# Retention values and the next unit's scores in one run of 64-row matmuls, with the values' results in the banks of the first products

## The chip, the cores and the metric

The kernel runs on one core of one Trainium2 chip. The metric is the device time of one execution in microseconds. A core has TensorE (PE in the rows, its weight loads PEld), VectorE (DVE), ScalarE (ACT), GpSimd (POOL) and SyncE (SP), which issues most DMAs here. Each engine works through its own queue in program order. TensorE writes only to PSUM, which has eight banks of 2 KB for each of its 128 partitions.

## The reference, cut to what matters

```python
scores = scale * np.matmul(q, k.transpose(0, 1, 3, 2))      # 4 x 8 heads, 576 tokens, dim 64
ret = scores * Dmat                                         # decay gamma**(i - j), causal
attn_out = np.matmul(ret, v)
x = attn_out.transpose(0, 2, 1, 3).reshape(2304, 512)
h = x @ w_in;  x = (h * sigmoid(h)) @ w_out                 # first layer, 512 -> 2048 -> 512
h = x @ w_in2; out = np.maximum(h, 0) ** 2 @ w_out2         # second layer
```

All of it is float32.

## The kernel before, in words

The 2,304 tokens are 18 units of 128. The retention of a unit is computed in chunks of 64 tokens: scores inside a chunk, a running state from chunk to chunk, and the values from both. Units 0 to 3 come first, by themselves. The other fourteen (4 to 17) are computed beside the first layer's ordinary products, which run in three blocks of 512, 384 and 384 tokens (j = 0, 1, 2). The remaining tokens and the second layer follow later with other products.

The first layer of one block is a loop over sixteen slices f of the hidden dimension. For each f, `gemm1` issues twelve 128x128 matmuls into one bank `ph`, ScalarE takes the Silu of it (line 743) and rounds it (745), VectorE forms the rest (746), and two slices later `gemm2` adds twelve matmuls into the four banks `acc`. So TensorE's order is gemm1(f), gemm2(f-2), gemm1(f+1), gemm2(f-1), and so on. A product keeps float32 precision by three matmuls for each pair: high by high, high by low, low by high.

The loop's body is cut into half steps n = 2f and n = 2f+1. At an even n the queue of TensorE stands between gemm1(f) and gemm2(f-2); at an odd n it stands between gemm2(f-2) and gemm1(f+1). In each half step the weights' conversion comes first (`conv_step` in block 0, `pre_step` in block 1: ScalarE's lines 126, 127 and 194, VectorE's 179, 182, 130 and 199), then `flush()`, which issues what the lists `later` and `behind` hold (the Silu at an even n, line 746 at an odd one), then gemm2 at an odd n, then `run_att`. ScalarE's order in an even half step of block 0 is therefore: the rounding of a converted weight (194), which waits for VectorE's line 130, and then the Silu.

`run_att` spreads two kinds of steps over the half steps by a proportion. `scores_step(u)` issues 64 matmuls on 64x64 tiles into the tile `P` (lines 442 and 446), then the state's additions (475, 477), the scaling of the queries (458) and the mask (450). `values_step(u)` issues 48 or 64 such matmuls into `Q` (496, 498, 504), copies one part of the result (506), and leaves the additions (527, 529 or 518, 520), the rounding (530) and the low part (534) for the next flushes. It then scales the keys of the next unit (`prep_k`: POOL's line 428 for the first half of the heads, four ScalarE instructions of line 431 for the second) and loads unit u+2 (line 406, from SP's queue).

In PSUM, `ps_a` has one tile of two banks, which `P` and `Q` take in turn; `ps_g` has two tiles of one bank, which the successive `ph` take in turn; `ps_o` has the four of `acc`.

```python
        at = behind if u < u_end[2] else later
        at.append(lambda: (whole(), at.append(low)))
...
                run_att(a0 + (a1 - a0) * (2 * f + odd + 1) // (27, 29, 22)[j])
```

With these numbers the steps of block 0 stand at n = 4 (scores of 4), 8 (values of 4), 13 (scores of 5), 17 (values of 5), 22 (scores of 6) and 26 (values of 6); those of block 1 at 4, 9, 14, 19, 24 and 28; those of block 2 at 1, 2, 4, 5, 6, 8, 9, 10, 12, 13, 15, 16, 17, 19, 20 and 21.

Of the kernel before, what the change touches and what calls it, by code (L numbers as in the profile page):

```python
# [7 lines left out]
F32 = mybir.dt.float32  # L8
# [15 lines left out]
NU = NCH  # L24
# [5 lines left out]
LAG = 2  # L30
W1_FIRST, SINGLES = 4, 6
HALVED = (7, 9)
AHEAD = 256
HALF = (slice(0, 64), slice(64, 128))
WARM = 5
# [8 lines left out]
def kernel(  # L44
# [147 lines left out]
    def pair_c(n, parts=slice(0, 2)):  # L192
        cols = slice(512 * parts.start, 512 * parts.stop)
        nc.scalar.copy(flat(tiles_of(*pairs[n - SINGLES])[0])[:, cols], conv[n][0].bitcast(F32)[:, cols])
# [8 lines left out]
    later = []  # L203
    behind = []
# [23 lines left out]
    def conv_step(n):  # L228
# [14 lines left out]
        if odd:  # L243
            if first < q <= end:
                parts = slice(1, 2) if q - 1 in HALVED else slice(0, 2)
                pair_c(q - 1, parts)
# [8 lines left out]
        if first < q <= end:  # L255
            if q - 1 in HALVED:
                for e in range(2):
# [87 lines left out]
    u_end = [sum(BLOCKS[: j + 1]) // C for j in range(len(BLOCKS))] + [NU]  # L345
# [3 lines left out]
    n_start = BLOCKS[0] // C  # L349
# [43 lines left out]
    def att_psum(name, pool=ps_a, tag="a"):  # L393
        return pool.tile([128, 2, 512], F32, tag=tag, name=name)

    def new_raw(u):
        if u < n_start:
            raw[u] = [wp.tile([128, 1024], F32, tag="w", name="raw") for _ in range(NG)]
        else:
            raw[u] = [ap.tile([128, 1024], F32, tag="raw", name="raw") for _ in range(NG)]  # L400

    def load(u, queue=nc.sync):
        if u < NU:
            new_raw(u)
            for g in range(NG):
                queue.dma_start(out=raw[u][g], in_=att[NG * u + g])
# [6 lines left out]
    def toks(u, a, e, b, first):  # L413

        c0 = first + (2 * a + e) % 4 * D
        return raw[u][a // 2][HALF[b], c0 : c0 + D]

    def place(u, b):

        return (2 * u + b) % PER  # L420

    def prep_k(u):

        for g in range(NG):
            kn = raw[u][g][:, 256:512].rearrange("p (h d) -> p h d", h=4)
            w = (Tkn_u if u < n_start else Tkn)[:, 4 * g : 4 * g + 4]
            if u == n_start or g == 0:
                nc.gpsimd.tensor_mul(kn, kn, w.unsqueeze(2).to_broadcast([128, 4, D]))
            else:
                for h in range(4):  # L430
                    nc.scalar.activation(kn[:, h], kn[:, h], ACTF.Copy, scale=w[:, h : h + 1])
# [3 lines left out]
    def scores(u):  # L435

        P_of[u] = P = att_psum("P")
        for a in range(4):
            for e, b in FOUR:
                if place(u, b) < PER - 1:  # L440
                    o = P[HALF[e], b, 256 + a * D : 256 + a * D + D]
                    mm(o, toks(u, a, e, b, 256), toks(u, a, e, b, 512), start=True, stop=True)  # L442
        for a in range(4):
            for e, b in FOUR:
                o = P[HALF[b], e, a * L : a * L + L]
                mm(o, dims(u, a, e, b, 768), dims(u, a, e, b, 0), start=True, stop=True)  # L446
# [10 lines left out]
            w = Tq[:, 2 * g : 2 * g + 2].unsqueeze(2).to_broadcast([128, 2, 2 - b0, L])  # L457
            nc.gpsimd.tensor_mul(q, q, w)

    def scores_step(u):  # L460
        scores(u)
        new_state(u, 0)
        scale_q(u)
        mask(u)
        new_state(u, 1)
# [17 lines left out]
    def values(u):  # L483


        Q = att_psum("Q")
        o = Q[:, 0].rearrange("p (a t) -> p a t", a=4)
        x1 = Q[:, 1, 0:256].rearrange("p (a t) -> p a t", a=4)
        rf = rf_t.pop(u)
        states = [b for b in range(2) if place(u, b)]  # L490
        for a in range(4):
            for e, b in FOUR:
                v = toks(u, a, e, b, 512)
                if e == b:
                    w = o[HALF[e], a, b * L : b * L + L]
                    mm(w, v, rf[HALF[b], e, a], start=a == 0, stop=a == 3 and not states)  # L496
                else:
                    mm(x1[HALF[e], a], v, rf[HALF[b], e, a], start=True, stop=True)
        for b in states:
            for a in range(4):  # L500
                for e in range(2):
                    sg = S_at[2 * u + b][HALF[e], a]
                    w = o[HALF[e], a, b * L : b * L + L]
                    mm(w, sg, dims(u, a, e, b, 0), start=False, stop=a == 3 and b == states[-1])  # L504
        xs = ap.tile([128, 4, L], F32, tag="xs", name="xs", bufs=1)
        nc.scalar.copy(xs, x1)
        xh, xl = x_part(u)
        raw.pop(u)
        if xl is None:
            for e, p in enumerate(HALF):  # L510
                nc.scalar.copy(xh[p, :, e * L : e * L + L], o[p, :, e * L : e * L + L])

        def into_x():
            for e, p in enumerate(HALF):
                b = 1 - e
                t = slice(b * L, b * L + L)
                if place(u, b):
                    nc.vector.tensor_add(xh[p, :, t], o[p, :, t], xs[p])
                else:
                    nc.vector.tensor_copy(xh[p, :, t], xs[p])  # L520

        def whole():
            for e, p in enumerate(HALF):
                b = 1 - e
                oc = o[p, :, b * L : b * L + L]
                if place(u, b):
                    nc.vector.tensor_add(oc, oc, xs[p])
                else:
                    nc.vector.tensor_copy(oc, xs[p])
            nc.scalar.copy(xh, o)  # L530

        if xl is None:
            return into_x, lambda: None
        return whole, lambda: nc.vector.tensor_sub(xl, o, xh)

    def values_step(u):
        whole, low = values(u)
        at = behind if u < u_end[2] else later
        at.append(lambda: (whole(), at.append(low)))
        if u + 1 < NU:  # L540
            prep_k(u + 1)
        load(u + 2)

# [230 lines left out]
    low = behind  # L776
# [422 lines left out]
    load_w(SINGLES)  # L1199

    first_units()
    att_steps = [(u, step) for u in range(n_start, NU) for step in (scores_step, values_step)]
    pos = [0]

    def run_att(upto):
        while pos[0] < min(upto, len(att_steps)):
            u, step = att_steps[pos[0]]
            step(u)
            pos[0] += 1

    def att_end(j):
        return 2 * (u_end[j] - n_start)

    su_ctx.close()
    ps_g, ps_o = (
        ps_ctx.enter_context(
            tc.tile_pool(name=nm, bufs=n, space=bass.MemoryType.PSUM, reuse_waits="tile")
        )
        for nm, n in (("ps_g", 2), ("ps_o", 4))
    )  # L1220
# [51 lines left out]
    for i in range(len(seq) + LAG):  # L1272
        if i < len(seq):
            layer, j, f = seq[i]
            if i == 0:
                for c in ((0, AHEAD), (AHEAD, BLOCKS[0])):
                    for ff in range(2):
                        gemm1(layer, j, ff, *c)
            elif i > 1:
                gemm1(layer, j, f)  # L1280
            if i == 0:
                for n in range(W1_FIRST):
                    keep_w(n)
            if i == 1:
                load(n_start + 1)
        for odd in range(2):
            if i == 0 and not odd:
                cut_consts(2)
            step = 2 * (i - (nb - 1) * KF) + odd
            if step >= 0:  # L1290
                flush()
            if i < len(seq):
                if j == 0:
                    conv_step(2 * f + odd)
                if j == 1 or step == 0:
                    pre_step()
                if j == 1 and odd == 0:
                    nc.sync.dma_start(out=woD[f // 2, f % 2], in_=w_pair[1, f // 2][f % 2].bitcast(F32))
            if step < 0:
                flush()  # L1300
            if odd and i >= LAG:
                gemm2(*seq[i - LAG])
            if i < len(seq):
                a0, a1 = att_end(j), att_end(j + 1)
                run_att(a0 + (a1 - a0) * (2 * f + odd + 1) // (27, 29, 22)[j])
                if j == nb - 1:
                    for p in range(5):
                        ts_step(p, step - 4 * p - 3)
            if step >= 0:
                strassen_x(step)  # L1310
    flush()
    flush()
    low = later
# [34 lines left out]
    for n in range(2 * KF):  # L1348
        h, f = divmod(n, KF)
# [11 lines left out]
        low = behind  # L1361
        last_block(n)
        low = later
# [55 lines left out]
    for n, (P, i) in enumerate(order2):  # L1419
# [8 lines left out]
        else:  # L1428
            at = 3 if P == 1 else 0
# [11 lines left out]
    low = []  # L1441
# [93 lines left out]
```

## Time and profile before

| | |
|---|---|
| median of three runs | 816.18 us (815.82 to 816.43) |
| the profiled execution's own time | 816.38 us |
| its span, first to last instruction | 814.6 us |
| outside the span | 1.8 us |
| TensorE busy | 805.3 us, 99% of the span |
| VectorE, ScalarE, POOL busy | 67%, 53%, 25% |
| granted TensorE clock, mean | 1.000 |

The blocks with the fourteen units lie between about 26 us and 290 us of the span; block 0 ends at about 120 us and block 1 at about 198 us. TensorE's busy time counts matmuls that overlap in its pipeline, so the order and the starts of its instructions tell more than that share.

### The profile page before, as it was taken

How to read it: one execution, taken by the hardware profiler on the slowest of the kernel's cores; microseconds unless marked ns; L12 is line 12 of the kernel's file. 1: busy time of each engine (PE TensorE's matmuls, PEld its weight loads, DVE VectorE, ACT ScalarE, POOL GpSimd, SP SyncE). 2: the span in 40 equal slices, each digit the busy share in tenths (PEclk: the TensorE clock that was granted, in tenths of full speed). 3: DMA queues.
4: the chain of work that ended last, by engine and by line, in shares of the span. 5: the costliest groups of instructions: out<-in, count | busy, mean ns of one | idle time of the engine just before them, and what ended most of it. 6: DMA issues, size and time to landing. Idle time of an engine off the chain costs nothing.

```text
span 814.6 us, 16076 instructions
## 1 busy us (share of the span) xinstructions
PE 805.3 (99%) x6426; PEld 747.6 (92%) x6426; DVE 545.6 (67%) x783; ACT 434.3 (53%) x797; POOL 202.6 (25%) x224
## 2 busy tenths in 40 slices
PE   7999999999999999999999999999999999999998
PEld 6887889999999988888888999999999999999998
DVE  5999975454455566575787676536566988777772
ACT  5787755444454445454455575645568644333330
POOL 3402202424566122223431222402355000000000
PEclk9999999999999999999999999999999999999999
DMA  9976555896552032788794565353488744433300
GB/s 352 393 283 231 211 199 197 313 325 240 196 193 95 2 117 93 257 312 286 228 358 159 172 216 162 129 169 105 149 306 280 283 166 153 138 133 133 107 27 27
DMA packets 73307, 160.69 MB, mean 197 GB/s; under 512 B 6032, under 2 KB 37520, under 8 KB 73232
## 3 DMA queue, kind: packets, MB, share of 16 engines
q1 hardware_dynamic: 68480, 151.28, 53.3%
q10 hardware_dynamic: 4752, 8.39, 2.8%
q8 instruction: 50, 0.82, 0.4%
q14 instruction: 25, 0.20, 0.1%
HBM read 104.07 MB, written 55.57 MB: 196 GB/s over the span
## 4 chain that ended last, share of the span: by engine, by line
PE 91%; issue 3%; DVE 2%; ACT 1%; POOL 0%; DVEq 0%; POOLq 0%; ACTq 0%
PE acc L83 23%; PE pa L1092 13%; PE pa L1001 12%; PE ph L83 11%; PE pb L1092 10%; PE pb L1001 9%; PE pa L860 5%; PE pb L860 4%; PE Q L504 1%; PE P L442 1%; PE Q L496 1%; PE P L446 1%; DVE t L130 0%; ACT t L126 0%; DVE t L143 0%
## 5 line engine op out<-in xcount | busy, mean ns | idle before, releaser
L1092 PE MATMUL pa<-w2s,gl 128*128 128x256 f32 x864 | 108.1, 283 | 0.0
L1001 PE MATMUL pa<-xa,w1s 128*128 128x384 f32 x576 | 106.0, 336 | 0.0
L1092 PEld LDWEIGHTS pa<-w2s,gl 128*128 128x128 f32 x864 | 105.7, 192 | 0.0
L1001 PEld LDWEIGHTS pa<-xa,w1s 128*128 128x128 f32 x576 | 100.5, 188 | 0.1
L83 PE MATMUL acc<-gsl,wo 128*128 128x512 f32 x384 | 87.4, 390 | 0.0
L83 PEld LDWEIGHTS acc<-gsl,wo 128*128 128x128 f32 x384 | 72.1, 188 | 15.2
L790 ACT CAST gl<-gr 128x1024 fp32r<-128x1024 f32 (+1 forms) x57 | 55.7, 1002 | 52.1 <-DVE gr L1066 25.3
L1092 PE MATMUL pb<-w2s,gl 128*128 128x256 f32 x648 | 82.0, 283 | 0.0
L1001 PE MATMUL pb<-xa,w1s 128*128 128x384 f32 x432 | 81.1, 336 | 0.0
L1092 PEld LDWEIGHTS pb<-w2s,gl 128*128 128x128 f32 x648 | 79.6, 192 | 0.0
L1001 PEld LDWEIGHTS pb<-xa,w1s 128*128 128x128 f32 x432 | 75.5, 188 | 0.4 <-DVE u L1013 0.4
L83 PE MATMUL ph<-xh,wih 128*128 128x384 f32 (+2 forms) x200 | 70.8, 354 | 0.7 <-ACT sg L743 0.7
L791 DVE TENSOR_TENSOR gl<-gr,gl 128x1024 fp32r<-128x1024 f32 (+1 forms) x55 | 64.4, 1179 | 8.0 <-ACT gl L790 8.0
L83 PE MATMUL acc<-gh,woh 128*128 128x384 f32 (+1 forms) x192 | 69.3, 361 | 0.0
L83 PE MATMUL ph<-xl,wih 128*128 128x384 f32 (+2 forms) x200 | 69.2, 346 | 0.0
L83 PE MATMUL ph<-xh,wil 128*128 128x384 f32 (+2 forms) x200 | 69.2, 346 | 0.0
L83 PE MATMUL acc<-gh,wol 128*128 128x384 f32 (+1 forms) x192 | 67.9, 354 | 0.7 <-DVE wol L199 0.7
L83 PE MATMUL acc<-gl,woh 128*128 128x384 f32 (+1 forms) x192 | 67.8, 353 | 0.0
L746 DVE TENSOR_TENSOR gl<-sg,gh 128x384 fp32r<-128x384 f32 (+1 forms) x48 | 31.5, 658 | 45.9 <-ACT gh L745 45.9
L743 ACT ACTIVATE sg<-ph 128x384 f32<-128x384 f32 (+1 forms) x48 | 25.2, 524 | 62.9 <-PE ph L83 62.0
L126 ACT ACTIVATE t<-wr 128x512 f32<-128x512 f32 x64 | 42.7, 667 | 22.4 <-DMA wr<-w 18.2
L1013 DVE TENSOR_TENSOR u<-pb,s 128x384 f32<-128x384 f32 x48 | 26.0, 553 | 31.9 <-PE pb L1001 31.6
(156 smaller groups left out, 1514.2 us busy)
## 6 DMA issues: line engine op xcount, KB each, us to landing
wr<-w SPq DMA_DIRECT2D x64, 512.0 KB, 5.9
gD<-g SPq DMA_DIRECT2D x48, 384.0 KB, 2.7
gr<-gD SPq DMA_DIRECT2D x36, 512.0 KB, 4.4
raw<-att SPq DMA_DIRECT2D x34, 512.0 KB, 4.9
wo<-woD SPq DMA_DIRECT2D x16, 512.0 KB, 6.4
w2r<-w2c SPq DMA_DIRECT2D x14, 512.0 KB, 6.0
xq<-x SPq DMA_DIRECT2D x12, 384.0 KB, 5.2
out<-y ACTq DMA_DIRECT2D x17, 256.0 KB, 2.0
```

Of the source, the lines that this page charges most:

```text
L83: mm(o, a, b, start=first and i == 0, stop=last and i == n - 1)
L126: nc.scalar.activation(t.bitcast(F32), hi.bitcast(F32), ACTF.Abs, scale=2.0**-112)
L442: mm(o, toks(u, a, e, b, 256), toks(u, a, e, b, 512), start=True, stop=True)
L446: mm(o, dims(u, a, e, b, 768), dims(u, a, e, b, 0), start=True, stop=True)
L743: nc.scalar.activation(s, ph, ACTF.Silu)
L746: later.append(lambda: nc.vector.tensor_sub(gl, s, gh))
L790: nc.scalar.copy(dst[0], src)
L791: low.append(lambda: engine.tensor_sub(dst[1], src, dst[0]))
L860: mm(o, lhs, rhs, start=m == 0 and i in (0, 1, 4), stop=m == 5, skip_group_check=True)
L1001: mm(o, lhs, rhs, start=m == 0 and i in (0, 1, 4), stop=m == 5, skip_group_check=True)
L1013: nc.vector.tensor_add(st[nm], o, st["s1"])
L1092: mm(o, lhs, rhs, start=first, stop=m == NP - 1 and q == 2, skip_group_check=True)
```

## The change

The values of unit u and the scores of unit u+1 are issued at the same place, in one run of 64x64 tiles: the scores first at an even half step (`early`), the values first at an odd one. The values' results no longer use `ps_a` but two tiles of `ps_g`: `x1` takes the bank of the older `ph`, `o` that of the newer one, and the next two `ph` follow in these banks. The additions and the rounding (`whole`) are issued at once, the low part at the next flush. The load of unit u+2 is issued behind the values, before the rest. The half steps are written out: values at `VALUES_AT`, keys at `KEYS_AT`, the first scores at n = 4 of block 0.

```diff
+SCORES_AT = 4
+VALUES_AT = ((8, 17, 26), (9, 19, 28), (1, 4, 7, 10, 13, 16, 19, 21))
+KEYS_AT = ((6, 13, 22), (4, 14, 24, 31), (3, 6, 9, 12, 15, 18))
...
-    def scores_step(u):
-        scores(u)
+    def after_scores(u):
         new_state(u, 0)
         scale_q(u)
         mask(u)
...
-        Q = att_psum("Q")
-        o = Q[:, 0].rearrange("p (a t) -> p a t", a=4)
-        x1 = Q[:, 1, 0:256].rearrange("p (a t) -> p a t", a=4)
+        x1, o = (ps_g.tile([128, 512], F32, tag="g", name=nm) for nm in ("x1", "o"))
+        o = o.rearrange("p (a t) -> p a t", a=4)
+        x1 = x1[:, 0:256].rearrange("p (a t) -> p a t", a=4)
...
-    def values_step(u):
+    def values_step(u, early):
+        more = u + 1 < NU
+        if more and early:
+            scores(u + 1)
         whole, low = values(u)
-        at = behind if u < u_end[2] else later
-        at.append(lambda: (whole(), at.append(low)))
-        if u + 1 < NU:
-            prep_k(u + 1)
         load(u + 2)
+        whole()
+        if more:
+            if not early:
+                scores(u + 1)
+            after_scores(u + 1)
+        behind.append(low)
...
+    values_u, keys_u = iter(range(n_start, NU)), iter(range(n_start + 1, NU))
+
+    def run_att(j, n):
+        if j == 0 and n == SCORES_AT:
+            scores(n_start)
+            after_scores(n_start)
+        if n in VALUES_AT[j]:
+            values_step(next(values_u), n % 2 == 0)
+        if n in KEYS_AT[j]:
+            prep_k(next(keys_u))
...
-                a0, a1 = att_end(j), att_end(j + 1)
-                run_att(a0 + (a1 - a0) * (2 * f + odd + 1) // (27, 29, 22)[j])
+                run_att(j, 2 * f + odd)
```

## Rows read from the trace of the kernel before

**Rows 1.** The page, part 1: busy time, share of the span, instructions.
```profile
PE 805.3 (99%) x6426; PEld 747.6 (92%) x6426; DVE 545.6 (67%) x783; ACT 434.3 (53%) x797; POOL 202.6 (25%) x224
```

**Rows 2.** The chain that ended last, block 2: start us, us, what.
```profile
199.85 0.62 PE P L442 x32
200.94 2.29 PE ph L83 x12
203.23 0.20 PE Q L496 x2
203.43 0.01 PE Q L498 x2
203.44 0.04 PE Q L496 x2
...
203.85 0.92 PE Q L504 x32
204.77 2.28 PE acc L83 x12
207.06 2.08 PE ph L83 x12
```

**Rows 3.** Timeline of TensorE, block 0: start us, us, engine, line, out<-in [idle before <-releaser].
```profile
47.88 0.27 PE L496 MATMUL Q<-rf,raw 64*64 64x64 f32 x2
...
51.81 0.39 PE L83 MATMUL ph<-xh,wih 128*128 128x512 f32 x1
...
54.53 0.39 PE L83 MATMUL acc<-gh,woh 128*128 128x512 f32 x1
...
59.97 0.39 PE L83 MATMUL acc<-gh,woh 128*128 128x512 f32 x1
...
62.78 0.69 PE L442 MATMUL P<-raw 64*64 64x64 f32 x32
...
66.73 0.39 PE L83 MATMUL acc<-gh,woh 128*128 128x512 f32 x1
...
72.17 0.39 PE L83 MATMUL acc<-gh,woh 128*128 128x512 f32 x1
...
73.49 0.50 PE L83 MATMUL acc<-gh,wol 128*128 128x512 f32 x1 [0.70 <-DVE wol L199]
...
76.00 0.27 PE L496 MATMUL Q<-rf,raw 64*64 64x64 f32 x2
```

**Rows 4.** Timeline of ScalarE, block 0.
```profile
48.85 0.62 ACT L745 CAST gh<-sg 128x512 fp32r<-128x512 f32 x1
...
52.57 1.06 ACT L194 CAST wih<-t 128x1024 fp32r<-128x1024 f32 x1 [0.82 <-DVE t L130]
53.53 0.59 ACT L743 ACTIVATE sg<-ph 128x512 f32<-128x512 f32 x1
...
54.94 1.07 ACT L431 ACTIVATE raw<-raw,cs 128x64 f32<-128x64 f32 x4
...
77.66 0.59 ACT L743 ACTIVATE sg<-ph 128x512 f32<-128x512 f32 x1
```

**Rows 5.** Timeline of VectorE, block 0.
```profile
51.19 1.28 DVE L130 SCALAR_TENSOR_TENSOR t<-wr,t 128x512 int32<-128x512 int32 x2
...
60.43 0.69 DVE L534 TENSOR_TENSOR xl<-Q,xh 128x512 fp32r<-128x512 f32 x1
```

**Rows 6.** The loads of units (line 406) in block 2, issue to landing.
```profile
DMA to landing us min/median/max: 3.5/4.3/5.5
```

**Rows 7.** Timeline of ScalarE, block 2.
```profile
207.71 0.48 ACT L763 COPY y<-acc 128x384 f32<-128x384 f32 x1 [0.79 <-DVE y L763]
...
209.69 0.33 ACTq L765 DMA_DIRECT2D x<-y  x1
...
216.50 0.49 ACT L743 ACTIVATE sg<-ph 128x384 f32<-128x384 f32 x1 [0.19 <-PE ph L83]
```

**Rows 8.** Stretches of the start: length, PE busy (x), granted clock, DMA share, GB/s.
```profile
0.00:10.00 10.00, 7.70 (x64) 1.00 0.81 293
10.00:20.00 10.00, 8.03 (x158) 1.00 1.03 410
```

More of the change, by code (lines that the diff above doesn't have):

```diff
@@ L1201 @@
     first_units()
[L1202 to L1212, printed above, removed]
+    values_u, keys_u = iter(range(n_start, NU)), iter(range(n_start + 1, NU))
[7 more added lines that the diff above has]
+            prep_k(next(keys_u))
     su_ctx.close()
```

## The prediction

> **What bounds the kernel now.** I read the page's busy times first: TensorE is busy 99% of the span, the next engine 67% [rows 1]. Then the chain that ended last: through the three blocks it is TensorE's own instructions end to end, so time is won here by what its queue no longer holds and lost by what makes it wait. The third view, TensorE's timeline in block 0, shows the one place after 45 us where it waits: at 73.49 for VectorE's conversion of a weight, 0.70 us of idle time [rows 3].
>
> What one separate run of 64x64 tiles costs beyond its matmuls stands in the chain [rows 2]. A group of twelve 128x128 matmuls takes 2.08 us; the group right behind such a run takes 2.29 or 2.28, so the way back costs 0.21. The first pair inside a run takes 0.20 where a later pair takes 0.04, so the way in costs 0.16. Together 0.37 us a run.
>
> **The change part by part.**
>
> *Runs removed.* Before there are 28 runs (scores and values of 14 units). After there are 15: the first scores alone, then 13 joined runs and the last values alone. The scores of units 6 to 17 lose a run each on a gapless path: 12 x 0.37 = **-4.4 us**. I take the joint between scores and values inside a run at nothing: in the rows the step from line 498 to 504, other operands and the same tile size, has no gap [rows 2]. The run of unit 5's scores is counted below.
>
> *New wait: the values need both `ph` banks.* `o` takes the bank of the newest `ph`, so the first matmul of the values waits until ScalarE's Silu has read it. In blocks 1 and 2 that is cheap. The Silu starts within 0.1 us of its products' end (216.50, 0.49 long) [rows 7]; at odd steps gemm2's 2.08 us lie between, at even ones the scores. In block 0 ScalarE runs behind. At n = 8 gemm1(4) ends just ahead of 47.88, where the values now start [rows 3], but its Silu runs from 53.53 to 54.12, behind the rounding at 52.57 that waited 0.82 us for VectorE [rows 4], whose line 130 ends at 51.19 + 1.28 = 52.47 [rows 5]. Nothing of the change moves that chain earlier, since VectorE's order up to there is the same.
>
> Ahead of the values stand, at n = 8, the scores of unit 5. They need unit 5's keys, whose ScalarE part now comes at n = 6, behind the rounding that ends at 49.47; 1.07 us of keys [rows 4] make it 50.5. TensorE idles from 47.9 to 50.5, does the scores in about 1.1, and idles again until the Silu. The keys push ScalarE's queue by 1.07, of which the 0.82 of waiting takes up most: the Silu ends at 54.12 + 0.25, about 54.4. The values start at 54.4 in place of 47.88: **+6.5 us** (bounds: 54.12 gives 6.2, all 1.07 of the keys behind it gives 7.3).
>
> *What comes back in block 0.* The scores of unit 5 are now done inside that wait. At n = 13 they cost 66.73 - 59.97 = 6.76 where two plain groups take 2 x 2.72 (51.81 to 54.53) = 5.44 [rows 3]: **-1.3**. And a TensorE that comes 5 us later no longer waits for the weight at 73.49: from 72.17 to the values at 76.00 are 3.83 us where 59.97 to 62.78 shows 2.81: **-1.0** [rows 3]. VectorE itself loses under 1 us by waiting for the values at n = 8 (its additions now stand ahead of the next weights), less than TensorE's delay, so it doesn't become the bound again.
>
> *The same wait elsewhere in block 0.* At n = 17 the old Silu of gemm1(8) ended at 78.25 [rows 4] with TensorE at 76.00; TensorE is now there at about 80.1 (76.00 + 6.5 - 1.3 - 1.0), so it costs nothing. At n = 26 TensorE is later by about as much, and scores come first; nothing.
>
> *The way out of the banks.* The next gemm1 waits for the copy of `x1` (line 506), the one after for the last reader of `o`: in blocks 0 and 1 the low part (534, 0.69 us [rows 5]), issued one flush later. At n = 8 I put the low part's end at 63.4, behind the mask, the state and a weight's conversion, and gemm1(6) at 63.8: nothing, with up to 0.7 if it slips by its own length. Units 10 and later have no low part. The additions and the rounding, now issued at once, make VectorE and ScalarE wait for TensorE; in block 1 both have idle time there.
>
> *Loads and keys.* SP issues the load as soon as the values are done, as before; behind it wait weight loads, 2.5 us later once (n = 8), needed 10 us on. In block 2, where a unit now takes three half steps, the tightest case is values at an odd step: from their end to the next scores' need are 0.9 of scores, 2.28 and two groups of 2.08, so 7.3 us [rows 2]. The two loads, the second issued about 0.5 later, land at most 5.5 after issue [rows 6], and the keys take 1.07: 7.1. It fits, barely; 0. One step doesn't: at n = 3 of block 2 ScalarE also evacuates the last results of block 1. Before, that evacuation ran until 210.02 [rows 7], 5.25 after its group began at 204.77 [rows 2]; with 1.07 of keys 6.3, and the scores of unit 12 want them after two groups, 2.28 + 2.08 = 4.4. That would be a wait of 2.0. At the other end, with both copies (0.48) and their issues packed tightly behind the products, 0.1. Before, the chain there began with 0.79 us of waiting for a VectorE copy, which came behind the additions of unit 10's values; these are now two half steps earlier. I take **+0.7**.
>
> *POOL* does the same work as before at other places; its scaling at n = 4 to 13 of block 0 is outside TensorE's path once TensorE is late.
>
> **The sum**: -4.4 + 6.5 - 1.3 - 1.0 + 0.7 = +0.5. The profiled execution took 816.38, its span 814.6 and 1.8 around it; it is 0.2 over the median. On the median: 816.18 + 0.5 = **816.7 us**. With the lower ends (6.2, 0, 0.1) 815.8, with the upper (7.3, 0.7, 2.0) 819.5.
>
> **Weighed against the trace: the clock.** The granted clock is 1.00 in all stretches I asked for, also in the first two of 10 us, where TensorE was busy 7.70 and 8.03 of 10 [rows 8]. But the new stretch from 47.9 to 54.4 would have it busy a good 1 us of 6.5, sparser than any stretch shown, so the rows bound the effect only from one side. The Trainium skill, page "TensorE: Matmul & The Clock Gate", section "A second HAM failure mode: psum-queue depth-cycling", says that a kernel whose TensorE idled briefly between groups of matmuls as it cycled through PSUM banks lost its full clock again and again. By the rows the sum stays 816.7; by that rule it goes to the second rival's time.
>
> **Rivals.**
> 1. *Faster: the bank wait is hidden.* If the values at n = 8 don't hold TensorE back (the Silu of gemm1(4) done by 49), the 6.5 and what it gives back fall away: -4.4 - 0.4 for unit 5's run = 811.4. For it: VectorE sets TensorE's time at 73.49, so a short wait before would cost nothing. Against it: 53.53 is a start seen in the trace, 5.6 us after the bank was filled. Between the two: with the other terms as they are, a wait below 4.3 us would still end under 814.5.
> 2. *Slower: the clock falls during the wait at n = 8.* At 1.2 GHz in place of 2.4 a group of twelve takes 2.72 more; one such group gives 819.4, two 822.1. It decides as soon as the sparse 6.5 us cost half a group. For it: the sparseness. Against it: 1.00 in every row.
> 3. *Slower: keys late in block 2.* If landing and keys take 8.3 in place of 7.1, the scores at n = 10 and 16 wait 1.0 each, those at n = 4 1.0 in place of 0.7, and those at 7, 13 and 19, which have 0.7 more room since the values come first, 0.3 each: +3.2, 819.9. For it: only 0.2 of room at the odd steps. Against it: 5.5 is the longest landing, the median is 4.3.
>
> **How the numbers follow.** About 0.2% (1.6 us) is what a measurement of this kernel can tell from no change, so "same" is 814.5 to 817.8. The sum as worked out has 0.65; 0.12 of it lies above 817.8 and 0.02 below 814.5. Rival 1 has 0.12 (0.1 faster, the rest same), rival 2 0.13, rival 3 0.10 (0.07 slower). Together faster 0.12, same 0.56, slower 0.32. The range from 814.8 to 819.7 leaves out most of rival 1 and the worse half of rivals 2 and 3.
>
> **What would show it.** Right: values at n = 8 starting near 54.4 with two idle stretches of about 2.6 us before and behind the scores of unit 5, ended by ScalarE (431, then 743); no wait at 73; 15 first pairs of 0.20 and 15 long groups behind them; the values of unit 5 at about 80.1 in place of 76.00, and the end of block 2 nearly where it was; one wait below 2 us at n = 4 of block 2. Wrong: a granted clock below 1 near 50 us; waits of TensorE for line 506 or 534, or for line 431 in every third half step of block 2; the joint inside a run costing as much as a changeover (0.37 x 13 = 4.8, which would give 821.5); or a bank wait of clearly less than 6 us.

## The result and the profile after

The changed kernel takes **821.18 us** (median of 6 runs, 820.71 to 821.54), the kernel before 816.01 beside it (6 runs, 815.72 to 816.43). The ratio is 1.0062 (95% interval 1.0049 to 1.0075): slower by 0.6%, 1.5 us above the top of the predicted range. In the profiled executions the spans are 818.9 and 814.6, so there are **+4.3 us** to find in them where the prediction had +0.5. (The medians lie 5.2 apart: the profiled execution of the changed kernel, 820.71, was the fastest of its six. What the others add is traced nowhere here.) Lines are shifted: scores stand at 445 and 449, values at 498, 500 and 506, the keys at 431 (GpSimd) and 434 (ScalarE), the Silu at 753, VectorE's part behind it at 756, the copies of `acc` into `y`, the block's results, at 773.

One slip in the sections ahead of the prediction: in the kernel before, the scores of unit 7 stand at n = 31 of block 0, not at n = 4 of block 1. No number of the prediction uses it.

The page, busy times and the row of the granted clock (40 slices of 20.5 us), answers [rows 1]:

```profile
PE 804.2 (98%) x6426; PEld 749.9 (92%) x6426; DVE 545.3 (67%) x783; ACT 436.2 (53%) x797; POOL 203.8 (25%) x224
...
PEclk9989999999999999999999999999999999999999
```

TensorE's busy time is 1.1 below before and its share fell: most of the extra time is waiting. The 8 in the third slice (41 to 61 us) is a clock that was not full. TensorE's timeline there, which answers [rows 3]:

```profile
47.76 0.46 PE L445 MATMUL P<-raw 64*64 64x64 f32 x16
49.65 1.09 PE L445 MATMUL P<-raw 64*64 64x64 f32 x13 [1.43 <-ACT raw L434]
...
51.40 0.50 PE L498 MATMUL o<-rf,raw 64*64 64x64 f32 x3
54.05 0.37 PE L500 MATMUL x<-rf,raw 64*64 64x64 f32 x2 [2.14 <-ACT sg L753]
...
55.75 0.79 PE L86 MATMUL acc<-gh,woh 128*128 128x512 f32 x1
...
59.22 0.39 PE L86 MATMUL ph<-xh,wih 128*128 128x512 f32 x1
...
81.08 0.27 PE L498 MATMUL o<-rf,raw 64*64 64x64 f32 x2
```

At n = 8 there are the two forecast idle stretches, ended by ScalarE's keys and then by its Silu; the values go on at 54.05 (47.88 before, 54.4 forecast). The matmul that waits is one of `x1`'s (the rows leave off the number of a name); `o`'s first had gone ahead from 51.3 on, before the Silu of the newest `ph`. So `x1` lies in the newer bank and `o` in the older one, the other way round than the section on the change and the prediction have it; experiment 4 shows the same. The values need both banks, so the wait is the same. Between 72.17 and 81.08 nothing waits any more: the stall at 73.49 is gone. ScalarE in the same place, which answers [rows 4]:

```profile
48.11 0.59 ACT L753 ACTIVATE sg<-ph 128x512 f32<-128x512 f32 x1
...
49.26 1.06 ACT L434 ACTIVATE raw<-raw,cs 128x64 f32<-128x64 f32 x4
...
52.48 1.03 ACT L197 CAST wih<-t 128x1024 fp32r<-128x1024 f32 x1
53.41 0.58 ACT L753 ACTIVATE sg<-ph 128x512 f32<-128x512 f32 x1
```

The Silu at 48.11 empties the older bank, the one at 53.41 the newer. The second holds the values; it starts 5.7 us after its products' end. And the clock, which [rows 8] showed at 1.00 in the start of the kernel before (stretch, length, TensorE's busy time, granted clock, DMA share, GB/s):

```profile
48.00:50.00 2.00, 0.57 (x22) 1.00 0.47 191
50.00:52.00 2.00, 1.91 (x50) 0.56 0.00 0
52.00:54.00 2.00, 0.00 (x0) 0.50 0.40 162
54.00:56.00 2.00, 1.95 (x45) 0.50 0.28 109
56.00:58.00 2.00, 2.00 (x7) 0.73 0.52 182
```

TensorE ran at 1.2 GHz (0.50) from about 50 to 57 us. Block 2, where [rows 2] had an unbroken chain:

```profile
204.40 0.27 PE L498 MATMUL o<-rf,raw 64*64 64x64 f32 x2
...
206.88 0.45 PE L86 MATMUL ph<-xh,wih 128*128 128x384 f32 x1
...
213.32 0.46 PE L445 MATMUL P<-raw 64*64 64x64 f32 x16
214.94 1.00 PE L445 MATMUL P<-raw 64*64 64x64 f32 x13 [1.16 <-ACT raw L434]
...
217.78 0.44 PE L86 MATMUL acc<-gh,woh 128*128 128x384 f32 x1
...
251.92 0.69 PE L445 MATMUL P<-raw 64*64 64x64 f32 x32 [1.30 <-POOL raw L431]
...
262.80 0.62 PE L445 MATMUL P<-raw 64*64 64x64 f32 x13 [0.32 <-POOL raw L431]
...
294.86 0.62 PE L870 MATMUL pa<-xsa,wih 128*128 128x512 f32 x2
```

A joined run without a wait (n = 1) lasts 206.88 - 204.40 = 2.48 us; the one at n = 4 lasts 217.78 - 213.32 = 4.46, so 1.98 more; the runs at n = 16 and 19 wait 1.30 and 0.32. All three are waits for keys, 3.6 us together. ScalarE ahead of n = 4, which answers [rows 7]:

```profile
212.17 0.48 ACT L773 COPY y<-acc 128x384 f32<-128x384 f32 x1 [1.86 <-DVE y L773]
...
213.60 0.48 ACT L773 COPY y<-acc 128x384 f32<-128x384 f32 x1 [0.96 <-PE ph L86]
...
214.54 1.06 ACT L434 ACTIVATE raw<-raw,cs 128x64 f32<-128x64 f32 x4 [0.46 <-ACT y L773]
```

The keys start at 214.54, after the scores' first matmul at 213.32. The copy at 212.17 waited 1.86 for VectorE's y copies, the one at 213.60 waited 0.96. VectorE in the same place:

```profile
210.34 0.89 DVE L756 TENSOR_TENSOR gl<-sg,gh 128x384 fp32r<-128x384 f32 x1 [1.03 <-ACT gh L755]
211.15 1.01 DVE L773 COPY y<-acc 128x384 f32<-128x384 f32 x2
```

Its y copies stand behind line 756, which waited 1.03 us for ScalarE's rounding of the last Silu. GpSimd ahead of n = 16:

```profile
248.07 1.05 POOL L832 TENSOR_TENSOR tss<-tsr 128x256 f32<-128x256 f32 x1
...
251.26 0.61 POOL L431 TENSOR_TENSOR raw<-raw,cs 128x256 f32<-128x256 f32 x1
```

Its half of the keys stands behind four weight sums of the next stage, which took it from 248.07 to 251.26.

### The profile page after: what moved, and what is told of

Its sections match the earlier page's. It is cut to its first block, busy times and chain, and to the rows that moved or that the text cites. A ratio compares the mean times of both kernels' runs of the same rounds, so it can differ in the third digit from the quotient of the medians.

```text
span 818.9 us, 16085 instructions
## 1 busy us (share of the span) xinstructions
PE 804.2 (98%) x6426; PEld 749.9 (92%) x6426; DVE 545.3 (67%) x783; ACT 436.2 (53%) x797; POOL 203.8 (25%) x224
## 4 chain that ended last, share of the span: by engine, by line
PE 91%; POOL 1%; DVE 1%; ACT 1%; DMA 1%; issue 1%; SPq 0%; ACTq 0%; POOLq 0%; DVEq 0%
PE acc L86 23%; PE pa L1102 13%; PE pa L1011 12%; PE ph L86 12%; PE pb L1102 9%; PE pb L1011 9%; PE pa L870 5%; PE pb L870 4%; PE o L506 1%; DMA wr<-w 1%; PE P L445 1%; PE o L498 1%; PE P L449 1%; POOL raw L461 0%; PE x L500 0%
```

## The experiments

Theory A: +6.2 from the bank wait at n = 8 and the half clock that follows it, and 3.6 from late keys in block 2; the joined runs themselves bring what was forecast. The main rival B: the joined runs or the new banks cost time everywhere, or the two holes are hidden by work elsewhere. The interval of a ratio is 0.001 to 0.002 to either side. Where the intervals of two kernels overlap (experiments 2 and 7 with the changed kernel, 5 with 1, 6 with 5 and with 8), their times alone don't tell them apart, and the waits in the profiles carry the argument.

**1. Block 0 apart.** The values of units 4 to 6 go back to a `ps_a` tile, and scores, values, keys and loads of block 0 to their old places; the joined runs begin with the values of unit 7.

```diff
 def values(u):
...
-    x1, o = (ps_g.tile([128, 512], F32, tag="g", name=nm) for nm in ("x1", "o"))
+    if u < u_end[1]:
+        Q = att_psum("Q")
+        o, x1 = Q[:, 0], Q[:, 1]
+    else:
+        x1, o = (ps_g.tile([128, 512], F32, tag="g", name=nm) for nm in ("x1", "o"))
...
+    def apart_step(u):
+        whole, low = values(u)
+        behind.append(lambda: (whole(), behind.append(low)))
+        prep_k(u + 1)
+        load(u + 2)
...
+            if n in (4, 13, 22, 31):
+                u = {4: 4, 13: 5, 22: 6, 31: 7}[n]
+                scores(u)
+                after_scores(u)
+            if n in VALUES_AT[0]:
+                apart_step(next(values_u))
+            return
```

> The change, but in block 0 the values of units 4 to 6 go back to a tile of the two-bank pool, with scores, values, keys and loads at the places of the kernel before; joined runs only from unit 7's values on (10 of 13). Theory A (the loss of block 0 is the values' wait for the Silu of the newest first product, with the clock's fall in it; each joined run gives 0.37; the rest is keys that come late in block 2): block 0 takes what it took before, so about 4.4 us less than the change, near 816.7. Rival B (values in the first products' banks cost something in every joined run, about 5.1 / 13 = 0.4 each): three of thirteen undone, near 820.0.

Measured 816.58 us (10 runs), ratio to before 1.0001 (0.9991 to 1.0010): A. The clock is 1.00 throughout, and the 0.7 us wait for the weight conversion is back. So the net loss to before is made in block 0, 821.18 - 816.58 = 4.6 us. From the first products of block 1 (119.63) to the first of the next stage (290.15) are 170.52 us, where the kernel before has 290.52 - 120.03 = 170.49: ten removed runs and nothing gained, with the same three waits for keys in block 2. The two rows of the kernel before:

```profile
120.03 0.45 PE L83 MATMUL ph<-xh,wih 128*128 128x384 f32 x1
...
290.52 0.62 PE L860 MATMUL pa<-xsa,wih 128*128 128x512 f32 x2
```

**2. Keys of block 2 earlier**, the rest as in the changed kernel.

```diff
-KEYS_AT = ((6, 13, 22), (4, 14, 24, 31), (3, 6, 9, 12, 15, 18))
+KEYS_AT = ((6, 13, 22), (4, 14, 24, 31), (2, 6, 9, 12, 14, 17))
```

> The change with only the keys of block 2 elsewhere: half steps 2, 6, 9, 12, 14, 17 in place of 3, 6, 9, 12, 15, 18, so that unit 12's stand ahead of the evacuation on ScalarE and unit 16's and 17's ahead of the weight sums on POOL. Theory A: the waits before the scores of units 12 (2.0), 16 (1.3) and 17 (0.3) go, 3.6 less, near 817.6. Rival B (loss spread over all runs) and rival C (these waits are the loads' landing, which this doesn't move): near 821.2.

Measured 819.48 (10 runs, 818.13 to 823.15), ratio 1.0044 (1.0031 to 1.0057): -1.7 against the changed kernel, about half of A's -3.6. The waits for keys are gone, but at n = 4 another took their place. ScalarE, then TensorE:

```profile
212.81 0.35 ACT L434 ACTIVATE raw<-raw,cs 128x64 f32<-128x64 f32 x1 [1.89 <-DMA raw<-att]
...
215.19 0.48 ACT L773 COPY y<-acc 128x384 f32<-128x384 f32 x1 [0.96 <-PE P L449]
...
216.07 0.49 ACT L753 ACTIVATE sg<-ph 128x384 f32<-128x384 f32 x1 [0.40 <-ACT y L773]
```
```profile
216.62 0.27 PE L500 MATMUL x<-rf,raw 64*64 64x64 f32 x2 [1.42 <-ACT sg L753]
```

Now the keys come ahead of the y copies, and the Silu that empties the values' bank comes behind them. Whichever of the two ScalarE does last, TensorE waits for it. In block 0 the wait for the Silu was 2.8 us in this profile instead of 2.1; -3.6 + 1.4 + 0.7 = -1.5, which is the difference of the spans (817.4 and 818.9).

**3. The wait at n = 8 filled with small matmuls**: the scores' matmuls of unit 5 issued several times over (288 extra ones, overwritten by the last).

```diff
 def scores(u):
...
+        if u == n_start + 1:
+            for _ in range(5):
+                qk()
+            for _ in range(2):
+                state()
+                qk()
+        state()
+        qk()
```

`state` and `qk` are the two halves of the scores' matmuls (lines 445 and 449 of the changed kernel).

> The change with TensorE kept busy while it waits at half step 8: unit 5's score products are issued five more times before its keys are there, and both parts of its scores twice more behind (288 more 64x64 matmuls, all into the same tile). Theory A (the granted clock fell to half because TensorE did little between 47.8 and 54 us, and that costs about 1.2): clock 1.00 through 48 to 58, the values of unit 4 again at 54, run and group behind it 1.2 shorter, near 820.0. Rival: the clock falls all the same, or its fall cost nothing: near 821.2 or above.

Measured 825.03 (4 runs), ratio 1.0103 (1.0083 to 1.0123): neither. The filler made a hole of its own: TensorE waited for nothing that the profile shows, 0.88 and 2.43 us, among the many small instructions (timeline), and the clock fell after that (stretches):

```profile
52.43 0.39 PE L446 MATMUL P<-raw 64*64 64x64 f32 x10 [0.88 <-issue]
...
56.98 0.27 PE L512 MATMUL x<-rf,raw 64*64 64x64 f32 x2 [2.43 <-issue]
```
```profile
54.00:56.00 2.00, 0.56 (x36) 1.00 0.29 104
56.00:58.00 2.00, 1.02 (x28) 1.00 0.01 2
58.00:60.00 2.00, 2.00 (x6) 0.53 0.59 168
```

The bank wait itself is gone in this run: the Silu ended at 54.00 and `o`'s first matmul started at 54.01. With holes of its own the run says nothing about the price of the clock at n = 8, so it was done again as experiment 7.

**4. The banks alone in block 0**: experiment 1, but with the values of units 4 to 6 in the two `ps_g` banks.

```diff
-    if u < u_end[1]:
-        Q = att_psum("Q")
-        o, x1 = Q[:, 0], Q[:, 1]
-    else:
-        x1, o = (ps_g.tile([128, 512], F32, tag="g", name=nm) for nm in ("x1", "o"))
+    x1, o = (ps_g.tile([128, 512], F32, tag="g", name=nm) for nm in ("x1", "o"))
```

> As e1_block0_apart, but the values of units 4 to 6 stay in the first products' banks: the bank wait alone, without joined runs and early keys in block 0. Theory A (the wait is for the Silu of the newest first product, which ScalarE reaches at 53.5 us behind the weight conversion): one idle stretch of about 6.2 at half step 8, of which 1.0 comes back at 73 us, and the clock falls: 6.4 more than e1, near 823.1. Rival D (what holds TensorE at half step 8 is the early scores and keys of unit 5, not the bank): as e1, near 816.7.

Measured 824.58 (4 runs), ratio 1.0100 (1.0083 to 1.0117): A, though more than forecast: +8.0 over experiment 1, from the choice of the bank and nothing else. TensorE at n = 8, then ScalarE there:

```profile
48.27 0.33 PE L498 MATMUL o<-rf,raw 64*64 64x64 f32 x4 [0.92 <-ACT sg L759]
53.57 0.37 PE L500 MATMUL x<-rf,raw 64*64 64x64 f32 x2 [4.97 <-ACT sg L759]
```
```profile
47.63 0.59 ACT L759 ACTIVATE sg<-ph 128x512 f32<-128x512 f32 x1
...
52.93 0.59 ACT L759 ACTIVATE sg<-ph 128x512 f32<-128x512 f32 x1
```

`o` starts when the first of the two Silus ends (48.22), `x1` when the second ends (53.52). With 0.7 more at n = 26 TensorE waits 6.6 us for the Silu. The half clock that follows (0.50 to 0.67 from 50 to 58 us) adds about 1.7: the rest of the run takes 1.70 us where experiment 7 below has 0.97, and gemm2 3.80 where it has 2.85. The wait at 73 us, 1.0 with what hangs on it, falls away. Together that is 7.3 of the 7.6 us by which block 1 starts later than in experiment 1 (127.24 against 119.63). In the changed kernel scores stand ahead of the values at n = 26 and nothing waits there, so the joined run's scores do hide that wait.

**5. Both remedies**: experiment 1 with the keys of experiment 2.

```diff
-KEYS_AT = ((6, 13, 22), (4, 14, 24, 31), (3, 6, 9, 12, 15, 18))
+KEYS_AT = ((6, 13, 22), (4, 14, 24, 31), (2, 6, 9, 12, 14, 17))
```

> e1_block0_apart and e2_keys_earlier together. Theory A (the two losses lie in different places and add): 1.7 less than e1, as the keys alone gave, near 814.9, with the wait at half step 4 of block 2 still there (for the Silu, which stands behind the evacuation on ScalarE) and those at 16 and 19 gone. Rival B (a cost in every joined run): nothing further gained, 816.6.

Measured 814.82 (11 runs), ratio 0.9983 (0.9975 to 0.9992): A. At n = 4 the wait for the Silu remains, 1.30 us.

**6. Evacuation of block 1 issued by SP**: experiment 5, with ScalarE relieved of the y transfers.

```diff
-queue = nc.sync if j == len(BLOCKS) - 1 else nc.scalar
+queue = nc.sync if j else nc.scalar
```

> e5_apart_and_keys, and the four result DMAs of block 1 issued from SP's queue in place of ScalarE's. Theory A: what held the Silu at half step 4 of block 2 were ScalarE's DMA issues, which waited for VectorE's copies; without them the run there goes through, 1.6 less than e5, near 813.2, and ten joined runs at 0.37 give 3.7 against the kernel before, 812.7. Rival: the wait stays (SP holds the issues or the loads behind them), as e5, near 814.9.

Measured 814.07 (6 runs), ratio 0.9970 (0.9958 to 0.9983): between the two. The wait at n = 4 is gone, but a new one stands at n = 7. SP's queue, then TensorE:

```profile
206.94 3.29 SPq L785 DMA_DIRECT2D x<-y  x4
...
211.07 1.94 SPq L409 DMA_DIRECT2D raw<-att  x2
```
```profile
220.04 0.75 PE L445 MATMUL P<-raw 64*64 64x64 f32 x6 [0.56 <-ACT raw L434]
```

The load of unit 13 stands behind y's transfers in SP's queue; it landed up to 7.0 us after its issue, and its keys held the scores. The issue itself was not later than in experiment 8 (211.07 against 210.93, landing there after at most 5.7), so it is the landing that was late; why is not shown, beyond what a change of the transfers' queue did.

**7. The wait filled with long matmuls**: the changed kernel with 15 matmuls of 128x512 and one more round of unit 5's scores at n = 8, all overwritten by the scores proper.

```diff
 def scores(u):
...
+        wait = u == n_start + 1
+        if wait:
+            for i in range(10):
+                mm(P[:, i % 2], wt[0, 0][0][:, 0:128], x_t[0][0][:, 0, 0:512], start=True, stop=True)
+            once(u, P)
+            for i in range(5):
+                mm(P[:, i % 2], wt[0, 0][0][:, 0:128], x_t[0][0][:, 0, 0:512], start=True, stop=True)
+        once(u, P)
```

> As e3_wait_filled, but with few long fillers: ten 128x512 matmuls ahead of unit 5's scores at half step 8, then the scores once more and five such matmuls, all into the scores' tile. In e3 the many small matmuls brought waits for instructions (0.88 and 2.43). Theory A: no such waits, the granted clock stays 1.00, the values of unit 4 start near 54.1 as in the change and the run and the group behind it take 1.2 less, near 820.0. Rival: the clock falls all the same, near 821.2.

Measured 822.63 (4 runs), ratio 1.0076 (1.0063 to 1.0090): no gain in the whole. At n = 8 itself A holds: the clock is 1.00 in every stretch from 46 to 64 us, and TensorE's timeline reads

```profile
54.57 0.27 PE L510 MATMUL x<-rf,raw 64*64 64x64 f32 x2 [0.35 <-ACT sg L763]
...
55.54 0.50 PE L86 MATMUL acc<-gh,woh 128*128 128x512 f32 x1
...
58.39 0.39 PE L86 MATMUL ph<-xh,wih 128*128 128x512 f32 x1
```

From the end of the bank wait to gemm2 are 0.97 us (54.05 to 55.75 = 1.70 in the changed kernel), and gemm2 lasts 2.85 (55.75 to 59.22 = 3.47). So the half clock cost 0.73 + 0.62 = **1.35 us**. But block 2 was worse in this run: its loads landed later (median 4.9 us against 4.2 in blocks 1 and 2 of the changed kernel), the waits for keys were 1.7 (n = 4), 2.0 and 0.3, and behind the first of them the clock fell again:

```profile
214.00:216.00 2.00, 0.83 (x14) 0.90 0.71 255
216.00:218.00 2.00, 2.00 (x78) 0.50 0.00 0
```

The 1.35 is shown where it arises; that it would come off the whole time is not shown by a median.

**8. Evacuation of block 1 issued by GpSimd**: experiment 6 with another queue.

```diff
-queue = nc.sync if j else nc.scalar
+queue = (nc.scalar, nc.gpsimd, nc.sync)[j]
```

> The kernel with block 0's joints apart, keys of block 2 earlier and the y transfers of block 1 issued by the y queue of SP (814.07) keeps a run at n = 7 of block 2 of 3.68 us where a free one takes 2.55, because the load of unit 13 stands behind y's transfers in SP's queue, and 0.4 at n = 19. Here those transfers are issued by GpSimd, which is idle from 206.9 to 213.4 in that kernel. My theory (the keys' waits in block 2 are all a matter of what stands ahead of the key work or of its load in one engine's queue): the run at n = 4 still goes through, the run at n = 7 drops to about 2.6, and the time to 812.7. Rival: GpSimd waits for y before each of its transfers and itself becomes late, so that its share of the keys and the scaled q of units 12 and 13 come later; then the waits move to POOL's key line and the time stays at 814 or above.

Measured **812.42** (5 runs, 812.17 to 812.67), ratio to before 0.9951 (0.9938 to 0.9965): A (812.7 was forecast), and faster than both kernels; block 0 and its banks are as in the kernel before. From 195 to 295 us TensorE has no wait left, and the next stage begins at

```profile
286.16 0.62 PE L880 MATMUL pa<-xsa,wih 128*128 128x512 f32 x2
```

Block 1 starts at 119.59, so the two blocks take 166.57 us, 3.9 less than the 170.49 of before. Ten runs of 0.37 are 3.7. The run at n = 4 goes through and the keys no longer wait, so what held them was what stood ahead of them, or of their load, in one engine's queue.

## Why the prediction was wrong

Two terms failed: the keys of block 2, put at +0.7, cost 3.6, and the fall of the clock, left out of the sum as a rival, cost 1.35.

**The sum as measured** in the profiled executions: runs removed -4.4, bank wait +6.2, unit 5's run -1.3, the wait at 73 gone -1.0, half clock +1.35, late keys in block 2 +3.6. That makes +4.45; the spans differ by 4.3. The +1.35 is a difference between two profiles and the rest is read from rows, so a tenth either way means nothing. It also closes stage by stage. Up to block 1 only the runs of units 6 and 7 count: 6.2 + 1.35 - 1.3 - 1.0 - 0.74 = 4.5, and block 1 starts at 124.48 instead of 120.03, 4.45 later. Blocks 1 and 2: -3.7 + 3.6 = -0.1, and the stage behind them starts at 294.86 instead of 290.52, 4.34 later.

**Right.** The 0.37 us of a run and the free joint inside one: experiment 8 gets the ten runs back in full once nothing waits. The bank wait at n = 8: place, cause and size (54.05 against 54.4; experiment 4 shows the bank alone makes it). Only the bank's name was wrong (`x1`, not `o`, waits for the newest `ph`), and the keys did not push the Silu back (53.41 against 53.53 before), so the wait came out at the lower bound, 6.2. What comes back in block 0: values of unit 5 at 81.08 against about 80.1, and the half clock is the difference. Rival 1, the hidden bank wait, is excluded.

**Wrong, first: "Loads and keys".** The step for n = 4 of block 2 took +0.7 of bounds 0.1 to 2.0; it measured 1.98. I had reckoned that the additions' earlier place would free VectorE for its y copies. The additions were out of the way, but line 756 now stood ahead of the copies and waited 1.03 us for ScalarE's rounding, so ScalarE waited 1.86 us for the copies (0.79 in [rows 7]). The keys started 5.5 us after the last group of block 1 began (209.07); the forecast's upper bound had 5.25 for that. And "It fits, barely; 0" for the other steps measured 1.6. At n = 16 ScalarE's keys did wait for the load until 249.71, but the last to come was GpSimd's half, behind the weight sums: the step counted landing and ScalarE's 1.07 us and never looked at what GpSimd's queue holds there, and "the same work at other places" is where that was passed over. Together the term made 2.9 of the 3.8 us that were missed (3.6 measured, 0.7 forecast). Rival 3 named 3.2 for late keys, nearly the size, but from late landings; experiments 2 and 5 removed the waits at 16 and 19 by moving the keys' place in the queues alone.

**Wrong, second: "Weighed against the trace: the clock".** The fall was given 0.13 as rival 2 although no row resembled the new stretch: [rows 8] have TensorE busy 77% and 80% of the time, the stretch from 48 to 50 us 28%. It happened. The Trainium skill, page "TensorE: Matmul & The Clock Gate", section "A second HAM failure mode: psum-queue depth-cycling", tells of a TensorE that idles briefly and often between groups of matmuls and whose clock goes down and up again. This trace agrees in kind, with one fall: an idle stretch of 1.43 us for keys, one of 2.14 for a PSUM bank, and a clock of 0.50. The price of the fall was half of what rival 2 put, 1.35 and not 2.72: the clock was back at about 57 us, during gemm2. It added 1.35 to the sum; without it the time would have come out at 821.18 - 1.35 = 819.8, still just above the range. Without the 2.9 of the keys it would have been 818.3, inside it. The prediction's 816.7 with both terms as measured gives about 821.

**What stays open.** The 0.9 us by which the medians lie further apart than the spans. The share of the clock in the whole time (experiment 7 did not show it in the median), and how far block 2's waits move from run to run with the loads' landing, which were 3.4 to 8.7 us in blocks 1 and 2 of the changed kernel's profile and 3.5 to 6.5 in experiment 7's.

## What to carry to other kernels

A result that moves into a bank which another engine must first empty inherits the lateness of that engine: read when the old reader ends, not how long it takes. Where two pieces of work of one engine both hold the next run of matmuls (here keys and Silu around an evacuation), moving one ahead can only swap the wait; take the third thing, the transfers' issue and its waits, off that engine. When a step is moved, write out the queue of every engine that does a part of it, the least busy one too: GpSimd is busy 25% of the span and still came last.

## What the runs showed of the hardware

In the changed kernel the granted clock fell to 0.50 although no idle stretch was longer than 2.14 us. In experiment 3 it was still 1.00 in two stretches of 2 us in which TensorE was busy 0.56 and 1.02 us, and 0.53 in the 2 us after them, with TensorE fully busy: the fall showed after the sparse stretches, not in them.

Going from 128x128 to 64x64 tiles and back cost 0.37 us a run by the rows of the kernel before; ten runs fewer gave 3.9 us back in experiment 8.

In experiment 3, among 288 extra 64x64 matmuls, TensorE stood for 0.88 and 2.43 us with nothing to wait for in the profile. Fewer and longer matmuls in the same place (experiment 7) showed no such wait. Instructions that came late would explain it: the profile's DMA view has a packet of the instruction queue near 50.1 us and one near 54.6 us, ahead of the ends of the two waits at 52.43 and 56.98 us, and 52 such packets in this run against 50 in the changed kernel. It is not shown, since no run changed that supply alone.
